# Six or eight rounded pieces of the second matrix beside the first layer of the first batch

## The chip, the cores and the metric

The kernel runs on one core of one Trainium2 chip. The metric is device time in microseconds of one execution; lower is better. All data are float32 except the two weight matrices, which arrive as float64.

## The reference

Eight batches of 448 rows pass through attention with 12 heads of 64, with normalised q and k, and then through two matrix products with a function between them.

```python
def _attn_ref(q, k, v, g_q, g_k):
    q_n, k_n = (rmsnorm(q, g_q), rmsnorm(k, g_k))
    scores = scale * np.matmul(q_n, k_n.transpose(0, 1, 3, 2))
    ...
    attn = attn / (np.sum(attn, axis=-1, keepdims=True) + 1e-09)
    return np.matmul(attn, v).astype(np.float32)

def _moe_ref(x, w_in, w_out):
    h = x @ w_in
    g = h - np.tanh(h)
    return (g @ w_out).astype(np.float32)
```

Here `x` is the attention output as 3584 x 768, `w_in` is 768 x 2048 and `w_out` is 2048 x 768.

## The kernel before

**Steps and batches.** One attention step handles two heads of one batch: 48 steps in all, six for each batch. While the attention of a batch is worked on, the two layers of the batch before it run beside it. The layers are a generator (`mlp`, L1273) that yields after each matmul; the attention code calls `run` (L1300) with a number of nanoseconds at fixed points of a step, and so many matmuls are written into the program there. `first_slot` (L1326) writes the steps of batch 0, `early_slot` (L1366) those of batch 1, beside which the first batch's layers run, and `slot` (L1394) the rest. The order within each engine's queue is the order of these calls; no scheduler changes it.

**The layers of batch 0.** The first layer (`hidden`, L865, through `products`, L813) multiplies by a scheme of seven products for each of four sets of weight blocks: 28 products of six matmuls of 128 x 224 each, in the order p = 1, 5, 6, 2, 3, 7, 4 within a set. Weight blocks 0, 1, 2 and 4 of a set are the weights themselves; blocks 5, 6, 3 and 7 are sums and differences of them, made on VectorE by `combine` (L354, the instructions of L356). The second layer of batch 0 (`project_first`, L1228) is plain: six groups of 16 matmuls of 128 x 448, counted by m from 0 to 95. The group is k = m // 16 and the row of the second matrix is f = m % 16. Groups k = 0 to 2 (below `HC`) use one half of the second matrix, groups 3 to 5 the other.

**Pieces of the weights.** The two float64 matrices are read as pairs of 32-bit words and rounded to float32 on the core, in 32 pieces of 768 KB: 16 of the first matrix (`CF`), then 16 of the second. Pieces 16 to 23 hold the half that the second layer's groups 0 to 2 need; row f needs piece 16 + f // 2. A piece passes through these steps, each on its own engine:

- `weight_load` (L278) issues its load on SyncE: four transfers at L289 for the first matrix, one at L293 for the second. Three buffers named `w_raw` take turns, so the load of piece n waits until piece n - 3 has been rounded.
- `round_weight_a` (L68): two ScalarE instructions, L71 and L72.
- `round_weight_b` (L75): three VectorE instructions, L78, L79 and L82.
- `round_weight_c` (L87): two GpSimd instructions at L92, one for each half of the piece; for the second matrix a half is one row f.

`weight(to)` (L320) rounds on until piece `to` - 1 has had its ScalarE part. For each piece n it issues `round_weight_a` of n, then `settle` (L335), which issues the VectorE and GpSimd parts of the piece before, then further loads, then up to two writes of finished blocks to DRAM (`keep_step`, L368, L371). `keep_w_out` (L392, L387) writes the rounded pieces of the second matrix back to DRAM as well.

**When pieces are due.** In the first layer the list `due` (L799) says for each of the 28 products how far the rounding must have come when the product is written (`product`, L822). If nothing is due, a pending VectorE and GpSimd part is settled and one block is written. In the second layer a formula in L1244 says it for each of the first 48 matmuls. Eight pieces are due before the first product (`EARLY`), 16 after 14 products, 24 after 28 products, and 32 after the first 48 matmuls of the second layer.

**What shares the queues.** A step of `early_slot` writes, in this order: the totals of the softmax (L696, with the reciprocal L701), scores of two chunks (L569) with their exponentials `p` (L575), the loads of v, a stretch of the layers, transposes of k and q (L467, L471) with their copies kT and qT on ScalarE (L469, L475) and two squarings (L132, L133), the loads of q and k, another stretch of the layers, scores of the last keys with the exponentials `p_last`, the values (L623, L673) with the division (L765), scores of one more chunk with the exponentials `p_full`, and then the norms (L142 to L144) and L454 between further stretches of the layers. Score banks are five in number and are used in turn, so the transposes use the bank of the totals again, and the second bank of the `p_full` scores is the first of `p_last`. The layers add their own work: tanh at L888, subtractions at L889 on VectorE or GpSimd, bank readers at L908 to L924, and in `project_first` a copy at L1264, a transpose at L950 and four output stores at L955.

Of the kernel before, what the change touches and what calls it, by code (L numbers as in the profile page):

```python
# [67 lines left out]
def round_weight_a(nc, raw, dst):  # L68

    lo, hi = raw[:, :, 0], raw[:, :, 1]  # L70
    nc.scalar.activation(dst, hi.bitcast(F32), AF.Abs, scale=2.0**-16)  # L71
    nc.scalar.mul(lo, lo.bitcast(U32), 2.0**-29)  # L72
# [74 lines left out]
def bounded_path(tc, ctx, q, k, v, moe_w_in, moe_w_out, out, g_col, ident, ones, half_ones, neg_half, early):  # L147
# [23 lines left out]
    CD, CF = DM // P, DFF // P  # L171
# [5 lines left out]
    EARLY, PIECES = 8, 2 * CF  # L177
    HS = S // 2
    HC, HF = CD // 2, CF // 2
    SETS = CF // 4  # L180
# [8 lines left out]
    def pool(name, **kw):  # L189
        return ctx.enter_context(tc.tile_pool(name=name, **kw))  # L190
# [23 lines left out]
    def mm_bank():  # L214
        return bank_of("mm")
# [48 lines left out]
    def w_out_row(f, i):  # L264
        return w_half[i][f // 2][:, f % 2]
# [35 lines left out]
    def weight_dst(n):  # L301
        return weight_piece(n)[2].rearrange("p f n -> p (f n)")
# [11 lines left out]
    def load_weights(to):  # L314

        while done[0] < min(to, PIECES) and place_free(done[0]):
            weight_load(done[0])
            done[0] += 1

    def weight(to):  # L320

        while done[1] < min(to, PIECES):
            n = done[1]
            keep_step(0, {CF - 4: 0, CF: 1, CF + HF: SETS - 1}.get(n, -1))
            round_weight_a(nc, raws[n], weight_dst(n))
            settle(n)
            done[1] = n + 1
            load_weights(n + (3 if n < EARLY - 3 else 4))
            if kept[1] < kept[0] and n >= 4 * kept[0] + 2:
                keep_weights()  # L330
            keep_step(2)
        if done[1] == PIECES:
            settle(PIECES)

    def settle(to):  # L335
        for n in range(done[2], to):
            round_weight_b(nc, raws[n], weight_dst(n))
            finish_weights(n + 1)
# [22 lines left out]
    def keep_weights():  # L361
        j = kept[1]
        to_keep.extend((j, p) for p in ORDER)
        kept[1] = j + 1
# [3 lines left out]
    def keep_step(count, all_of=-1):  # L368
        while to_keep and (count > 0 or to_keep[0][0] <= all_of):
            j, p = to_keep.pop(0)  # L370
            nc.sync.dma_start(out=w_in_dram[j, p].rearrange("p (f n) -> p f n", f=2), in_=built(j, p))  # L371
            count -= 1

    def combine_w_out(f):

        a11, a21 = (w_out_row(f, i) for i in range(2))
        a12, a22 = (w_out_row(f + HF, i) for i in range(2))
        t = [ring_slot() for _ in range(2)]
        s3, s1, s2, s4 = (t[i // 2][:, i % 2 * HALF : (i % 2 + 1) * HALF] for i in range(4))
        nc.vector.tensor_tensor(out=s1, in0=a21, in1=a22, op=ALU.add)  # L380
        nc.vector.tensor_tensor(out=s3, in0=a11, in1=a21, op=ALU.subtract)
        nc.vector.tensor_tensor(out=s2, in0=s1, in1=a11, op=ALU.subtract)
        nc.vector.tensor_tensor(out=s4, in0=a12, in1=s2, op=ALU.subtract)
        late["keep"].append(lambda: [keep_factors(3 + 2 * i, 2, f, t[i]) for i in range(2)])
# [7 lines left out]
    def keep_w_out(n):  # L392

        if not CF <= n < PIECES:
            return
        f, i, src = weight_piece(n)
        if f >= HF or i == 0:
            blk = i + 1 if f >= HF else 0
            for r in range(2):
                keep_factors(blk, 1, f % HF + r, src[:, r])  # L400
# [18 lines left out]
    def ring_load(to):  # L419

        for n in range(len(ring_tiles), min(to, len(ring_steps))):
            b, layer, j, p = ring_steps[n]
            t = ring_tiles[ring_steps[n]] = ring_slot()
            if layer == 0:
                assert kept[1] > j
                nc.sync.dma_start(out=t[:, : 2 * HALF], in_=w_in_dram[j, p])
            elif layer == 2 and p == 0:
                nc.sync.dma_start(out=t, in_=w_out_dram[:, BLOCKS[j], HC - 1].rearrange("p f d -> p (f d)"))
            elif layer == 2:
                n = min(2 * HB, 7 * HB - 2 * (p - 1) * HB)  # L430
                at = 2 * (p - 1) * HB
                nc.sync.dma_start(out=t[:, :n], in_=inner_dram[j][:, at : at + n])
            else:
                nc.sync.dma_start(out=t, in_=w_out_dram[:, BLOCKS[p], j].rearrange("p f d -> p (f d)"))
# [361 lines left out]
    late = {}  # L796


    due = [EARLY + (CF - EARLY) * (m + 1) // (7 * SETS // 2) for m in range(7 * SETS // 2)]  # L799
    due += [CF + HF * (m + 1) // (7 * SETS // 2) for m in range(7 * SETS // 2)]  # L800
    assert len(due) == 7 * SETS and due[-1] == CF + HF

    def part(name):
        if name == "th" and "blocks" in late:
            late["turn"] = (late.get("turn", 0) + 1) % 3
            if late["turn"] == 0:
                return late["blocks"].tile([P, 2, HS], F32, name="th_more")
        return tp.tile([P, 2, HS], F32, name=name)
# [134 lines left out]
    def store(b, n, y, o=None):  # L943

        if o is None:
            o = part("th").rearrange("p f s -> p (f s)")
        nc.vector.transpose(out=o, in_=y if b >= FIRST else y.rearrange("r (c p) -> r p c", c=NCH))  # L950

        def issue():
            for i in range(P // BL):
                d = n * P + i * BL
                nc.sync.dma_start(  # L955
                    out=out[b * S : (b + 1) * S, d : d + BL].rearrange("(j t) d -> t j d", t=BL),
                    in_=o[i * BL : (i + 1) * BL].rearrange("t (j d) -> t j d", d=BL),
                )

        late["out"].append([1 if b >= PAIRED else 2, issue])  # L960

    def step_out(by=1):
        for entry in late["out"]:
            entry[0] -= by
        while late["out"] and late["out"][0][0] <= 0:
            late["out"].pop(0)[1]()
# [261 lines left out]
    def project_first(b):  # L1228

        g = late["g"]  # L1230
        for fn in late["todo"]:
            fn()
        late["todo"] = []
        keep_step(0, SETS - 1)
        took = 4 * S / ENGINE_NS
        for m in range(CD * CF):
            k, f = m // CF, m % CF
            n = (k + HC) % CD
            if f == 0:
                bank = mm_bank()  # L1240
            if f == CF // 2:
                step_out(2)
            if k < HC:
                weight(CF + HF + HF * (m + 1) // (HC * CF))  # L1244
            elif m < HC * CF + 2:
                keep_w_out(PIECES - 2 + m - HC * CF)
            elif (m - HC * CF) % 4 == 0 and m - HC * CF <= 4 * HF:
                for fn in late["keep"]:
                    fn()
                late["keep"] = []  # L1250
                combine_w_out((m - HC * CF) // 4 - 1)
            elif m == CD * CF - 12:
                ring_load(2)
                for fn in late["keep"]:
                    fn()
            elif m == CD * CF - 10:
                ring_load(4)
            nc.tensor.matmul(  # L1258
                bank[:, :S], lhsT=w_out_row(f, n // HC)[:, n % HC * P : (n % HC + 1) * P], rhs=g[:, f, :],
                start=(f == 0), stop=(f == CF - 1),  # L1260
            )
            if f == CF - 1:
                y = part("s2").rearrange("p f s -> p (f s)")
                nc.scalar.copy(out=y, in_=bank[:, :S])  # L1264
                store(b, n, y)
            yield took
        wp_stack.close()
        late["blocks"] = pool("blocks", bufs=1)
        late["second"] = pool("second", bufs=1)
        late["tg"] = single_stack.enter_context(tc.tile_pool(name="tg", bufs=1))  # L1270
        late["inner"] = inner_steps()
# [415 lines left out]
def kernel(  # L1687
# [77 lines left out]
    with tc.If(bounded) as cmp:  # L1765
        with ExitStack() as arm, tc.manual_schedule():
            bounded_path(tc, arm, q, k, v, moe_w_in, moe_w_out, out, g_col, ident, ones, half_ones, neg_half, early)
# [34 lines left out]
```

## Time and profile before

| what | us |
|---|---|
| median of three runs | 1359.16 |
| lowest and highest run | 1357.87, 1359.49 |
| the profiled execution, its own time | 1356.19 |
| its span, first to last instruction | 1354.4 |
| TensorE matmul busy in the span | 1317.9 |
| VectorE, GpSimd, ScalarE busy | 949.1, 775.1, 556.9 |

The profile is of one execution, and instruction times in it count from the start of its span. Its own time is 1.8 us longer than the span, and it is 2.97 us shorter than the median of the three runs. In that execution the first layer of batch 0 begins at 76.8 us, its last product ends at 173.1 us, and the second layer runs from 176.4 us; its 49th matmul begins at 225.6 us.

In the stretches that the change touches, the engines were busy as follows:

| stretch, us | TensorE | VectorE | ScalarE | GpSimd | DMA share |
|---|---|---|---|---|---|
| 76 to 132 (first half of the first layer) | 49.1 of 56.0 | 53.4 | 32.2 | 33.6 | 0.81 |
| 132 to 176.4 (second half) | 44.4 of 44.4 | 41.7 | 25.1 | 34.8 | 0.89 |
| 176.4 to 221.3 (first half of the second layer) | 44.9 of 44.9 | 36.1 | 29.1 | 30.1 | 0.89 |

A row of the timeline gives start, duration, engine, line, operation, output and input; a bracket at its end tells how long the engine had been idle before it, and which instruction or transfer ended that.

### The profile page before, as it was taken

To read this page: it belongs to the slowest core of one execution; us is meant where nothing else is said; L and a number is where in the kernel's file an instruction comes from. 1 tells how busy PE (TensorE), PEld (TensorE's weight loads), DVE (VectorE), ACT (ScalarE), POOL (GpSimd) and SP (SyncE) were. 2 spreads that over 40 slices of the span, in tenths; PEclk is the share of its full clock that TensorE was granted. 3 is DMA by queue.
4 is the path that set the end of the run, shared out by engine and by line. 5 is a ranking of instruction groups with operands and counts; after the bars stand their busy time and mean duration, and the time that the engine had idled before them with its cause. 6 is when DMAs were issued, how large, how long until landed. Compare 5 with 4: busy or idle time off the path is not lost.

```text
span 1354.4 us, 29206 instructions
## 1 busy us (share of the span) xinstructions
PE 1317.9 (97%) x11336; PEld 1029.0 (76%) x11336; DVE 949.1 (70%) x1393; ACT 556.9 (41%) x1326; POOL 775.1 (57%) x591
## 2 busy tenths in 40 slices
PE   7989999999999999999999999999999999999996
PEld 3467854478998878697778787778787888699985
DVE  4999978757855768587887576768786668434453
ACT  7856654344433454445322446354512264311100
POOL 4766766347846256626698235844699253712761
PEclk9999999999999999999999999999999999999999
DMA  7879889889999667476655867476645775365544
GB/s 172 197 198 266 254 256 254 249 247 280 335 302 274 169 157 182 107 192 151 162 145 138 197 169 179 110 180 163 168 139 139 160 194 158 107 163 178 171 143 84
DMA packets 371688, 253.54 MB, mean 187 GB/s; under 512 B 282196, under 2 KB 310228, under 8 KB 371540
## 3 DMA queue, kind: packets, MB, share of 16 engines
q1 hardware_dynamic: 371536, 251.57, 68.9%
q8 instruction: 92, 1.51, 0.5%
q14 instruction: 56, 0.46, 0.1%
q10 hardware_dynamic: 4, 0.00, 0.0%
HBM read 205.23 MB, written 46.27 MB: 186 GB/s over the span
## 4 chain that ended last, share of the span: by engine, by line
PE 84%; DVE 9%; DMA 2%; SPq 2%; issue 1%; ACT 1%; POOL 1%; DVEq 0%; ACTq 0%
PE mm L841 36%; PE mm L1094 23%; PE sc L569 9%; PE sc L635 6%; PE mm L1258 5%; DVE xT L762 1%; PE sc L673 1%; PE sc L623 1%; SPq L955 1%; PE mm L673 1%; DVE rows L613 1%; DMA w_f<-w_in 1%; DVE rows L606 1%; DVE rows L600 1%; DMA w_f<-w_inner 0%
## 5 line engine op out<-in xcount | busy, mean ns | idle before, releaser
L841 PE MATMUL mm<-xT,w_f 128*128 128x224 f32 x1296 | 264.0, 353 | 0.7 <-DVE s L912 0.7
L841 PEld LDWEIGHTS mm<-xT,w_f 128*128 128x128 f32 x1296 | 244.5, 190 | 6.4 <-issue 4.8
L569 PE MATMUL sc<-qT,kT 64*32 64x448 f32 (+1 forms) x3072 | 214.2, 499 | 2.9 <-ACT p_last L575 1.7
L841 PE MATMUL mm<-tt,w_f 128*128 128x224 f32 x1044 | 213.7, 356 | 0.8 <-DMA w_f<-w_in 0.2
L841 PEld LDWEIGHTS mm<-tt,w_f 128*128 128x128 f32 x1044 | 194.9, 190 | 19.1 <-issue 15.4
L523 POOL TENSOR_TENSOR rr_mine<-rr_mine,neg_half 128x28 f32<-128x28 f32 x33 | 160.6, 4868 | 2.7
L758 DVE TENSOR_TENSOR xT<-xT,sc 128x448 f32<-128x448 f32 x32 | 19.9, 622 | 176.8 <-PE sc L569 119.3
L889 POOL TENSOR_TENSOR gT<-s,th 128x448 f32<-128x448 f32 x44 | 56.1, 1277 | 145.3 <-ACT th L888 142.0
L1094 PE MATMUL mm<-u,w_f 128*128 128x224 f32 x672 | 136.5, 354 | 1.2 <-DVE sum_all L733 0.9
L1094 PE MATMUL mm<-gT,w_f 128*128 128x224 f32 (+1 forms) x480 | 133.0, 429 | 3.1 <-DVE acc L1101 3.0
L1094 PEld LDWEIGHTS mm<-u,w_f 128*128 128x128 f32 x672 | 126.1, 190 | 8.2 <-POOL u L1051 3.9
L569 PEld LDWEIGHTS sc<-qT,kT 64*32 64x32 f32 x3072 | 71.0, 106 | 70.4 <-issue 50.5
L1094 PEld LDWEIGHTS mm<-gT,w_f 128*128 128x128 f32 x480 | 90.2, 190 | 40.7 <-issue 34.2
L635 PE MATMUL sc<-p,v_nat 64*32 64x448 f32 x1120 | 110.5, 536 | 0.0
L1094 PE MATMUL mm<-g,w_f 128*128 128x224 f32 (+1 forms) x360 | 99.5, 428 | 1.1 <-DVE acc L1101 1.1
L725 ACT COPY sum_g<-sum 32x14 f32<-32x14 f32 x280 | 56.3, 201 | 106.1 <-DVE sum L717 100.3
L889 POOL TENSOR_TENSOR g<-s,th 128x448 f32<-128x448 f32 x24 | 30.6, 1278 | 108.2 <-ACT th L888 93.3
L575 ACT ACTIVATE p<-sc 128x448 f32<-128x448 f32 x132 | 71.7, 543 | 50.3 <-PE sc L569 42.4
L1094 PEld LDWEIGHTS mm<-g,w_f 128*128 128x128 f32 x360 | 67.9, 190 | 28.2 <-issue 26.2
L1258 PE MATMUL mm<-gT,w_out 128*128 128x448 f32 x192 | 74.4, 543 | 0.0
L1051 POOL TENSOR_TENSOR u<-gT 128x448 f32<-128x448 f32 x48 | 58.8, 1247 | 11.1 <-PE mm L1094 11.1
L144 POOL TENSOR_TENSOR rr<-rr,neg_half 112x8 f32<-112x8 f32 (+1 forms) x30 | 49.4, 1675 | 26.7 <-DVE rr L143 26.2
(196 smaller groups left out, 2427.9 us busy)
## 6 DMA issues: line engine op xcount, KB each, us to landing
w_f<-w_in SPq DMA_DIRECT2D x196, 384.0 KB, 3.5
w_f<-w_inner SPq DMA_DIRECT2D x63, 512.0 KB, 3.7
w_f<-w_out SPq DMA_DIRECT2D x42, 512.0 KB, 3.9
w_raw<-in_moe_w_out_dram SPq DMA_DIRECT2D x16, 768.0 KB, 5.6
w_in<-w_out SPq DMA_DIRECT2D x21, 384.0 KB, 5.1
qk_nat<-in_q_dram SPq DMA_DIRECT2D x132, 56.0 KB, 2.8
qk_nat<-in_k_dram SPq DMA_DIRECT2D x132, 56.0 KB, 2.3
g<-w_out SPq DMA_DIRECT2D x14, 512.0 KB, 5.1
```

What stands on the lines that cost most here:

```text
L144: nc.gpsimd.tensor_tensor(out=r, in0=r, in1=neg_half[:rows], op=ALU.pow)
L523: nc.gpsimd.tensor_tensor(out=mine, in0=mine, in1=neg_half[:, :1].to_broadcast([P, 2 * NJ]), op=ALU.pow)
L569: nc.tensor.matmul(tiles[h][i * BL : (i + 1) * BL, :n], lhsT=kT[r, c * P + at : c * P + at + BL], rhs=qT[r, first : first + n], start=True ...
L575: nc.scalar.activation(p[:, h, c if c < 2 else 0, :], tiles[h][:, :n], AF.Exp, scale=1.0 if rr is None else rr[:, 0, 2 * c + h : 2 * c + h ...
L635: nc.tensor.matmul(av[g][i * BL : (i + 1) * BL, :S], lhsT=v_nat[keys, h, c, m * BL : (m + 1) * BL], rhs=p[keys, h], start=first, stop=True ...
L673: nc.tensor.matmul(av[n][r : r + BL, :HS], lhsT=v_nat[:, h, c, m * BL : (m + 1) * BL], rhs=p[c][:, h, n * HS : (n + 1) * HS], start=False, ...
L725: nc.scalar.copy(out=acc[h * BL : (h + 1) * BL, g], in_=part[g * BL : (g + 1) * BL, h * NJ : (h + 1) * NJ])
L841: nc.tensor.matmul(bank[:, f * HS : (f + 1) * HS], lhsT=w[:, c * width + f, :], rhs=moving[p](c), start=(first and f == 0 and c == 0), sto ...
L889: eng.tensor_tensor(out=g[:, rows, cols], in0=h, in1=th, op=ALU.subtract)
L1051: nc.gpsimd.tensor_tensor(out=u[:, half], in0=a[:, half], in1=z[:, half], op=ALU.subtract)
L1094: nc.tensor.matmul(bank[:, :n], lhsT=w(i), rhs=mv, start=(first and i == 0), stop=(i == len(moving) - 1), skip_group_check=not first,)
L1258: nc.tensor.matmul(bank[:, :S], lhsT=w_out_row(f, n // HC)[:, n % HC * P : (n % HC + 1) * P], rhs=g[:, f, :], start=(f == 0), stop=(f == C ...
```

## The change

Two lists of due times change. In the first layer the 14 pieces from the ninth on are spread evenly over the 28 products, so that 22 pieces are due at its end where 24 were. In the second layer a new list, `behind`, takes the place of the formula: ten pieces are due in its first 48 matmuls where eight were. For the first 16 matmuls the list also holds the rounding ahead of the rows: at matmul m it is at least 19 + m // 2.

```diff
-    due = [EARLY + (CF - EARLY) * (m + 1) // (7 * SETS // 2) for m in range(7 * SETS // 2)]
-    due += [CF + HF * (m + 1) // (7 * SETS // 2) for m in range(7 * SETS // 2)]
-    assert len(due) == 7 * SETS and due[-1] == CF + HF
+    SOME = HF - 2
+    due = [EARLY + (CF - EARLY + SOME) * (m + 1) // (7 * SETS) for m in range(7 * SETS)]
+    assert due[-1] == CF + SOME and due[7 * (SETS - 1) - 1] > CF
+    behind = [max(CF + m // 2 + 3, CF + SOME + (2 * HF - SOME) * (m + 1) // (HC * CF)) for m in range(CF)]
+    behind += [CF + SOME + (2 * HF - SOME) * (m + 1) // (HC * CF) for m in range(CF, HC * CF)]
...
             if k < HC:
-                weight(CF + HF + HF * (m + 1) // (HC * CF))
+                weight(behind[m])
             elif m < HC * CF + 2:
```

Here EARLY is 8, CF 16, HF 8, HC 3 and SETS 4. Pieces 0 to 10 are due where they were. Piece 11 is due at product 7 where it was due at 6, piece 16 at product 17 where it was at 15, piece 21 at product 27 where it was at 24, with products counted from 0. Pieces 22 and 23 were due at products 26 and 27 and are now due at matmuls 4 and 9 of the second layer; piece 24 was due at matmul 5 and is now due at 12, piece 25 at 11 and now at 14, and piece 31 stays at 47. The matmuls and their order are the same in both kernels.

## The prediction, on record before the result

> **What bounds the kernel now.** I read the page's busy shares first, then the chain of work that ended last in order of time, then the instructions around the change engine by engine. "Round a", "b" and "c" of a piece are lines 71 and 72 (ScalarE), 78 to 82 (VectorE) and 92 (GpSimd); a(25) is round a of piece 25.
>
> ```profile
> PE 1317.9 (97%) x11336; PEld 1029.0 (76%) x11336; DVE 949.1 (70%) x1393; ACT 556.9 (41%) x1326; POOL 775.1 (57%) x591
> ```
>
> TensorE is the bound nearly everywhere, so only its few stalls can be won or lost. In the stretch of the change the chain runs through VectorE up to 120.8 us and through TensorE after it (start, us, what):
>
> ```profile
> 109.53 1.78 DVE w_f L82
> 111.31 0.88 DVE w_f L356
> 112.21 1.66 DVE w_f L356
> ...
> 116.39 0.48 DVE w_out L78
> 116.89 0.57 DVE w_out L79
> 117.48 0.96 DVE w_out L82
> 118.44 0.87 DVE w_f L356
> 119.31 1.48 DVE rs L701
> 120.83 0.66 PE sc L467 x4
> ...
> 130.51 1.72 PE sc L569 x16
> ```
>
> The reciprocal L701 frees the bank that the transposes L467 need; TensorE stood still 2.32 us for it (its own row says so), because rounding b of piece 12 and three combinations L356 were ahead. The scores at 130.51 took 1.72 us where the same 16 took 0.92 at 98.00: their bank waited for an exponential behind a(15). From 132 us to the end of the first batch no row of TensorE shows idle before it until 275 us. What keeps that so is thin:
>
> ```profile
> 188.21 0.92 ACT L71 ACTIVATE w_out<-w_raw 128x768 f32<-128x768 f32 x1
> 189.02 1.05 ACT L72 ACTIVATE w_raw<-w_raw 128x768 int32<-128x768 uint32 x1
> 189.90 0.53 ACT L1264 COPY s<-mm 128x448 f32<-128x448 f32 x1
> 190.34 0.77 ACT L575 ACTIVATE p_last<-sc,rr 128x224 f32<-128x224 f32 x2
> ...
> 199.86 0.92 ACT L71 ACTIVATE w_out<-w_raw 128x768 f32<-128x768 f32 x1 [3.15 <-DMA w_raw<-in_moe_w_out_dram]
> ```
>
> Here a(25) runs without waiting and the exponentials p_last follow; a(27) at 199.86 waits for its load. The transfers, as SyncE issues them:
>
> ```profile
> 188.56 0.37 SPq L293 DMA_DIRECT2D w_raw<-in_moe_w_out_dram  x1
> 189.05 0.93 SPq L103 DMA_DIRECT2D qk_nat<-in_q_dram  x2
> ...
> 192.68 1.12 SPq L387 DMA_DIRECT2D w_out<-w_out  x2
> 193.97 1.15 SPq L293 DMA_DIRECT2D w_raw<-in_moe_w_out_dram  x1
> ```
>
> Load 26 at 188.56, six loads of q and k, two writes, load 27 at 193.97, used at 199.86: 11.3 us from one load's issue to the use of the next.
>
> **What the Trainium skill says.** "PSUM — Partial Sum Buffer", Engine vs sequencer instructions: the queues of ScalarE, VectorE and GpSimd are strict FIFO. The trace agrees: at 222.06 a(31) starts after 3.39 us of waiting for its load, and p_last, whose scores were done at 221.85, follows only at 224.17. "SBUF — State Buffer", Who interferes with whom: VectorE in a two-port mode or with two SBUF inputs and GpSimd lock each other out of a shared port pair. The trace agrees: L79 takes 0.56 us alone and 1.26 beside a GpSimd row, a half of round c 1.0 and up to 1.87. "DMA: Bandwidth & Descriptors", Anatomy of one DMA: 2.0 us plus bytes over 436 GB/s (fitted to another issuing path), an estimate of 3.8 us for a piece of 768 KB; the trace says 4.6 least, 5.6 median, 9.4 most from issue to landing, and decides.
>
> **The change part by part.** TensorE's own order is the same in both builds; all moves are on the other queues. Nothing is added or removed in all: each moved piece takes with it its load on SyncE, two ScalarE rows (1.8 us), three VectorE rows (2.1, up to 3.8 beside GpSimd), two GpSimd rows (2.0 to 3.3) and, for the second matrix, two writes. Up to the sixth product nothing moves; each later piece of the first 22 moves back by 1 to 3 products, and 22 and 23 leave the first layer.
>
> 1. *Gain at the transposes of 120.83.* Rounding b of piece 12 (116.39 to 118.44, 2.05) goes behind L701, and one of the three combinations (0.87 at least). L701 ends at 120.8 - 2.9 = 117.9 at the latest; TensorE is ready at 118.5. The wait of 2.32 us goes; late next are TensorE's own products. Cover: 0.6 us.
>
> 2. *Gain at the scores of 130.51.* a(15) goes behind p_last and p_full. p_last is then ready at about 128.0, where the scores come at 128.1 (130.51 - 2.3). Gain 1.72 - 0.92 = 0.8. Together -3.1 us.
>
> 3. *Hidden part, 132 to 176 us.* Seven pieces instead of eight; DVE 41.7, ACT 25.1 and POOL 34.8 of 44.4 us were busy, and TensorE did not wait. Moved with them past VectorE's and GpSimd's other rows are the combinations of set 3; the first is still some 10 us ahead of its product. On SyncE loads of v, q and k now stand before loads 15, 16 and 21; they have a whole step of some 30 us to land. The next reciprocal (149.58, needed at 151.7) gets more room. I cost this part at nothing; if that cover is gone, a late piece or reciprocal costs what the stall of 120.83 cost, up to 2.3.
>
> 4. *Loss at the first third of the second layer.* Four pieces, 22 to 25, are now issued in its first 16 products instead of two. Let T be the start of the transposes after the eighth product (182.53 before). a(23) now stands behind kT, qT and two squarings that need these transposes. In the next third such a group let a piece start at T + 2.64 (216.93 - 214.29). Then 0.9 (L71), b 0.56 + 0.56 + 0.96 = 2.1, and c in two halves of 1.0 to 1.6: done at T + 6.7 and T + 7.7 to 8.3. The products of rows 14 and 15 want them at T + 5.4 and T + 6.2: a wait of 1.5 to 2.1 us.
>
> 5. *Loss at the scores after it.* Load 24 must wait until round c of piece 21 frees the buffer. With U the end of the hidden products (T = U + 9.4): on GpSimd the power pair takes U to U + 3.3; three subtractions L889 follow, the last of which needs a tanh behind L454 (2.0), four exponentials (2.1) and itself (0.5), U + 6.3; it ends at U + 7.6 to 8.0; c(21) takes 2.0 to 2.6 (the 2.62 of 160.63). So load 24 is issued at T + 0.2 to T + 1.2; before it went out 9.6 us ahead of T. In the new SyncE order the six q and k loads and two writes stand between loads 24 and 25, as between 26 and 27 above: +11.3, a(25) starts at T + 11.5 to 12.5. Behind it on ScalarE wait L1264 and p_last: 1.67 + 0.45 + 0.40 = 2.5, first p_last ready at T + 14 to T + 15. The second scores bank is p_last's, wanted at T + 10.4 (192.93 - 182.53). Points 4 and 5 together cost 3.6 to 4.6 us with these landings, 2.5 with the shortest and 8 and more with the longest. I take 4.6, since rounding b of 21 and 22 runs just beside those GpSimd rows.
>
> 6. *Loss in the next third.* Load 29 (206.08 before, ahead of the output stores) falls behind four stores that need the bank finished at V (206.07 before): copy 0.5, transpose 0.9, stores 2.2, two writes 1.1, with waits V + 5.0. Load 31 goes out about when 29 has landed (each transfer waits for the eighth before it in this build): V + 11.7. It lands 5.7 later (216.30 to 222.06), then 2.5 as above: p_last at V + 19.9, wanted at V + 18.6 (224.63 - 206.07). Cost 1.3; zero to 4 with the landings. After that the pieces are done by 230 us, before their products, and the delay rides to the end.
>
> **Sum.** -3.1 + 4.6 + 1.3 = +2.8 us on the profiled execution: 1356.19 (span 1354.4, 1.8 around it) becomes 1359.0. The median of the runs lies 2.97 above that execution: 1359.16 + 2.8 = 1362.0.
>
> **Rivals.**
> *The loads come in time (ends not slower).* Loads 24 and 25 decide: if a(25) starts by T + 9.5, p_last is ready when the scores, already 1.6 late through point 4, come. That needs 8.3 to 9.3 us for the pair in place of 11.3; the shortest landing twice is 9.2, so c(21) must also end early. DMA engines were busy 0.83 in 176 to 201, so they have some room; the measured pair speaks against it. -3.1 + 1.6 + 0.2: 1357.9.
> *The gain alone.* Rounding a of 23 finds ScalarE so early that nothing waits: 1356.1. Against it: the order kT before a(23) is in the build.
> *The loads pile up.* 201 to 222 had DMA busy 0.97; landings of 7 to 9 us for loads 24, 25, 28 and 31 add 2 to 3 each twice on the way: +5.5 to +8, about 1366.
> *It doesn't do what it says:* the built order shows the pieces moved; no chance is given.
>
> **Chances.** The forecast 0.50 (1360 to 1364.5, of which 0.30 above the bound), pile-up 0.20, in time 0.18 (0.14 within), gain alone 0.12 (0.10 faster). The bound of 0.2% is 2.7 us, about what a measurement of this kernel can tell from no change. Slower 0.50, within 0.36, faster 0.14. The range from 1356.4 to 1367.0 leaves out some 0.08 below and 0.06 above.
>
> **What would show it.** Right: no idle of TensorE before the transposes near 118.5; an idle at the products of rows 14 and 15 with releaser GpSimd L92; one at the scores ten us after the transposes with releaser ScalarE p_last, and there a(25) with a long DMA wait; load 24 issued just after c(21). Wrong: a(25) without DMA wait; a new wait in 132 to 176; a stall that stays at 120.

## The result, and the profile after

The changed kernel takes 1361.9 us (median of 13 runs, 1360.12 to 1364.81). In the same series the kernel before took 1357.38 us (13 runs; the three shown above, with a median of 1359.16, are the first of them). The ratio is 1.0032, 95% interval 1.0025 to 1.0040: 4.3 us slower, 3.4 to 5.4. Here and below, microseconds beside a ratio are the ratio's; differences of medians can be up to 1.2 us off from them. The profiled execution has a span of 1358.7 us, against 1354.4.

The change did take away the stall that it met first. TensorE's rows after the change, with start, duration, engine, line, operation and, in brackets, the idle time before the row and who ended it:

```profile
118.15 0.60 PE L467 MATMUL sc<-ident,qk_nat 128*128 128x128 f32 x4
119.02 0.60 PE L471 MATMUL sc<-ident,n 112*128 112x112 f32 x4 [0.27 <-ACT p L575]
...
184.36 1.02 PE L1260 MATMUL mm<-gT,w_out 128*128 128x448 f32 x2 [0.30 <-POOL w_out L92]
186.91 1.99 PE L1260 MATMUL mm<-gT,w_out 128*128 128x448 f32 x4 [1.53 <-POOL w_out L92]
188.84 0.61 PE L569 MATMUL sc<-qT,kT 64*32 64x224 f32 x16
...
192.16 0.94 PE L569 MATMUL sc<-qT,kT 64*32 64x448 f32 x2
194.93 0.98 PE L569 MATMUL sc<-qT,kT 64*32 64x448 f32 x14 [1.83 <-ACT p_last L575]
195.84 1.02 PE L1260 MATMUL mm<-gT,w_out 128*128 128x448 f32 x2
```

The transposes L467 start at 118.15 with no bracket; before, they started at 120.83 behind 2.32 us of idle time. The loss follows 65 us later: two products wait for GpSimd's L92 (each product of the second layer is two matmuls in these rows; the one at 184.36 is that of row 13, for piece 22, and 186.91 begins rows 14 and 15, for piece 23), and 14 of the 16 scores for p_last. The sum of such waits from 135 to 285 us (engine, what waited, releaser, us in all, times, longest):

```profile
PE sc L569 <- ACT p_last L575: 2.5, 2, 1.8
PE mm L1260 <- POOL w_out L92: 1.8, 2, 1.5
PE sc L569 <- ACT p L575: 0.4, 1, 0.4
```

The kernel before has only the last of the three there, with 0.5. Where p_last was kept shows on ScalarE and SyncE. First ScalarE, then SyncE's queue:

```profile
186.20 0.90 ACT L71 ACTIVATE w_out<-w_raw 128x768 f32<-128x768 f32 x1 [2.53 <-DMA w_raw<-in_moe_w_out_dram]
...
192.45 0.90 ACT L71 ACTIVATE w_out<-w_raw 128x768 f32<-128x768 f32 x1 [4.55 <-DMA w_raw<-in_moe_w_out_dram]
193.26 0.86 ACT L72 ACTIVATE w_raw<-w_raw 128x768 int32<-128x768 uint32 x1
194.03 0.50 ACT L1266 COPY s<-mm 128x448 f32<-128x448 f32 x1
194.44 0.78 ACT L575 ACTIVATE p_last<-sc,rr 128x224 f32<-128x224 f32 x2
```

```profile
181.05 0.37 SPq L293 DMA_DIRECT2D w_raw<-in_moe_w_out_dram  x1
181.54 0.93 SPq L103 DMA_DIRECT2D qk_nat<-in_q_dram  x2
...
185.12 1.45 SPq L387 DMA_DIRECT2D w_out<-w_out  x2
186.72 0.40 SPq L293 DMA_DIRECT2D w_raw<-in_moe_w_out_dram  x1
```

Before, a(25) ran at 188.21 with no wait and p_last at 190.34. Now load 24 goes out at 181.05, load 25 at 186.72, a(25) starts at 192.45 after 4.55 us of waiting, and p_last stands behind it. The chain of waits of the changed kernel runs through just these (start, us, what):

```profile
186.72 5.70 DMA w_raw<-in_moe_w_out_dram
...
193.26 0.86 ACT w_raw L72
194.12 0.41 ACT s L1266
194.53 0.35 ACT p_last L575
...
194.93 0.98 PE sc L569 x14
```

A bracket shows less than a wait costs, because ends of matmuls are modelled. So I count delays from starts of rows. T is the start of the transposes after the eighth product of the second layer; before, the first scores start at T + 7.00 and the 17th product 4.24 us after them, and the 49th product 31.83 us after the 17th. What exceeds that is delay. "Second batch" is the start of the first eight of its products (277.80 before).

| us | before | after | change |
|---|---|---|---|
| products after the scores near 130 us | 132.16 | 129.10 | -3.06 |
| T | 182.53 | 179.30 | -3.23 |
| first scores (rows 14 and 15 waited) | 189.53 | 188.84 | +2.54 |
| 17th product (p_last waited) | 193.77 | 195.84 | +2.76 |
| 49th product (next third waited) | 225.60 | 229.10 | +1.43 |
| second batch | 277.80 | 281.30 | +3.50 in all |
| last long run of products | 1260.72 | 1264.89 | +4.17 in all |

The balance is -3.23 + 2.54 + 2.76 + 1.43 = +3.50. Another 0.7 us in all is lost later, where the change has no instruction: the changed kernel stands 3.1 us behind near 770 us and 4.2 near 1090 us.

### The profile page after: what moved, and what is told of

Its sections match the earlier page's. It is cut to its first block, busy times and chain, and to the rows that moved or that the text cites. A ratio compares the mean times of both kernels' runs of the same rounds, so it can differ in the third digit from the quotient of the medians.

```text
span 1358.7 us, 29209 instructions
## 1 busy us (share of the span) xinstructions
PE 1321.9 (97%) x11336; PEld 1030.2 (76%) x11336; DVE 951.3 (70%) x1393; ACT 557.9 (41%) x1326; POOL 771.2 (57%) x591
## 4 chain that ended last, share of the span: by engine, by line
PE 79%; DVE 9%; DMA 3%; SPq 2%; ACT 2%; issue 2%; POOL 1%; DVEq 0%; ACTq 0%; POOLq 0%
PE mm L843 35%; PE mm L1096 23%; PE sc L569 8%; PE sc L635 5%; PE mm L1260 4%; DVE xT L762 2%; DMA w_raw<-in_moe_w_in_dram 1%; DVE rows L613 1%; PE sc L623 1%; DMA w_raw<-in_moe_w_out_dram 1%; DVE rows L606 1%; DVE rows L600 1%; DVE sum_T L710 1%; PE sc L673 1%; ACT p L575 1%
## 5 line engine op out<-in xcount | busy, mean ns | idle before, releaser
L891 POOL TENSOR_TENSOR gT<-s,th 128x448 f32<-128x448 f32 x44 | 55.6, 1269 | 140.5 <-ACT th L890 140.0
L891 POOL TENSOR_TENSOR g<-s,th 128x448 f32<-128x448 f32 x24 | 30.3, 1264 | 108.8 <-ACT th L890 93.8
L1260 PEld LDWEIGHTS mm<-gT,w_out 128*128 128x128 f32 x192 | 35.4, 190 | 39.7 <-issue 34.1
```

The source lines that it names most:

```text
L891: eng.tensor_tensor(out=g[:, rows, cols], in0=h, in1=th, op=ALU.subtract)
L1260: nc.tensor.matmul(bank[:, :S], lhsT=w_out_row(f, n // HC)[:, n % HC * P : (n % HC + 1) * P], rhs=g[:, f, :], start=(f == 0), stop=(f == C ...
```

## The experiments

Ratios are to the kernel before on the same chip (1359.16 us for the first four, 1357.37 for the next four).

### Each half of the change alone

Here the first layer ends with 24 pieces as before and the second layer is untouched. The first 14 products have the due times of the change (15 pieces), and nine pieces are left for the other 14:

```diff
+    due = [EARLY + (m + 1) // 2 for m in range(7 * SETS // 2)]
+    due += [CF - 1 + (HF + 1) * (m + 1) // (7 * SETS // 2) for m in range(7 * SETS // 2)]
...
+                weight(CF + HF + HF * (m + 1) // (HC * CF))
```

> The first layer's list as changed for its first 14 products (15 pieces due), then nine pieces in the other 14, so that 24 are due at its end; the second layer is left as before. Theory (gain and loss are two separate things): the 3.2 us gained by 130 us stay, the transposes of the second layer start at about 179.3 against 182.5 before, and no exponential p_last is waited for. Rows 14 and 15 of the second layer may wait up to 2.5, since round c of piece 23 ended only 0.2 us before its product in the kernel before and hangs on its load. In all 0.5 to 3.2 us faster than before. Rival (the rounding costs TensorE time wherever it lies): the gain is given back in the second half of the first layer, transposes not before 181.5, and the time within 1 us of before.

Measured: 1357.0 us, ratio 0.9985 (0.9977 to 0.9992), 2.0 us faster than before. There is no delay at rows 14 and 15, at p_last or in the next third; the second batch starts at 276.08 (-1.72). The gain at 120 and 130 us can thus be had without the loss. It is not kept whole: the transposes of 118.15 come at 118.73 (TensorE was as far behind at 111 us already), and the scores of 158.72, which take 0.98 in the changed kernel, take 2.02 here, because a piece waited for its load ahead of p_last. ScalarE in this kernel:

```profile
157.57 0.97 ACT L71 ACTIVATE w_out<-w_raw 128x768 f32<-128x768 f32 x1 [0.85 <-DMA w_raw<-in_moe_w_out_dram]
158.44 0.95 ACT L72 ACTIVATE w_raw<-w_raw 128x768 int32<-128x768 uint32 x1
159.28 0.75 ACT L575 ACTIVATE p_last<-sc,rr 128x224 f32<-128x224 f32 x2
```

So nine pieces in the second half of the first layer do cost something, 1.0 us here; the rival had that part right. Eight cost little: the same scores took 1.16 us in the kernel before and 0.98 in the run with seven pieces of eight below, which also has eight pieces in that half.

The other half alone has the old first 14 due times and the new list in the second layer:

```diff
+    due = [EARLY + (CF - EARLY) * (m + 1) // (7 * SETS // 2) for m in range(7 * SETS // 2)]
+    due += [CF + SOME * (m + 1) // (7 * SETS // 2) for m in range(7 * SETS // 2)]
```

> The first 14 products as in the kernel before (16 pieces due), six pieces in the other 14, and the second layer as changed (ten pieces). Theory: no gain at 118 to 131 us, the whole loss in the second layer: waits of TensorE of about 1.8 at rows 14 and 15, 3.5 at the scores after them and 1.4 a third later, 6.7 us in all, so 5 to 7 us slower than before. Rival (the waits come from TensorE being 3.2 us ahead of the transfers, and are the gain given back): waits of 3.5 or less in all, and at most 3.5 us slower than before.

Measured: 1366.56 us, ratio 1.0057 (1.0042 to 1.0071), +7.7 us. The stall at 120.83 is back (2.61), and the delays are those of the changed kernel to 0.05 us: 2.54, 2.78, and 1.47 in the next third once 1.59 us are taken off that TensorE lost there at half clock (32 products took 13.88 us in place of 12.29). The gain and the loss are two things in two places. The timed halves, -2.0 and +7.7, come to 5.7 where the whole change has 4.3; their intervals, 1 and 2 us to either side, cover the difference.

### Is it p_last?

In the two steps concerned, TensorE's scores for p_last and its exponentials are written ahead of the eight products, so p_last stands ahead of the piece in ScalarE's queue:

```diff
+        if s in (9, 10):
+            scores(s + 1, KF)
         run(gap)
-        if has(s + 1):
+        if has(s + 1) and s not in (9, 10):
             scores(s + 1, KF)
```

> The changed kernel, but in the two steps beside the first half of the second layer the scores of the last keys and their exponentials p_last are written ahead of the second stretch of the layers, so that on ScalarE they stand before rounding a of pieces 23 to 25 and 30 to 31 and not behind it. Theory (the loss is p_last standing behind a piece whose load is late): the waits for p_last of 3.5 and 1.4 go, the wait at rows 14 and 15 grows by the 0.8 us that p_last takes on ScalarE, to about 2.6; the 49th matmul of the second layer starts near 225 against 229.1 in the changed kernel and 225.6 before; about 4 us faster than the changed kernel, within 1.5 of before. Rival (ten pieces are more than the engines and transfers carry in that time): the waits move to other instructions, and the time stays within 1.5 us of the changed kernel.

Measured: 1360.12 us, ratio 1.0006 (0.9997 to 1.0015), level with the kernel before. TensorE in this kernel:

```profile
187.26 2.00 PE L1260 MATMUL mm<-gT,w_out 128*128 128x448 f32 x4 [1.66 <-POOL w_out L92]
...
192.13 0.98 PE L569 MATMUL sc<-qT,kT 64*32 64x448 f32 x16
193.04 1.40 PE L1260 MATMUL mm<-gT,w_out 128*128 128x448 f32 x3
```

The wait for L92 is there (1.66); the 16 scores are one row again, with no bracket. The 49th product starts at 225.09, 4.0 us ahead of the changed kernel: about the 2.76 + 1.43 of p_last. The second batch starts at 277.87, 3.4 us ahead. Of the 0.6 us lost in between, 0.5 lie at the row sums L696 of 237.31, which took 1.10 us in place of 0.58: VectorE's L613, whose result they read, ended only at 237.78.

### Is it piece 23?

Piece 23 is due at the eighth product, ahead of the transposes, and load 25 stays where it was:

```diff
+    behind[7:9] = [CF + HF] * 2
...
-            load_weights(n + (3 if n < EARLY - 3 else 4))
+            load_weights(n + (3 if n < EARLY - 3 else 2 if n == CF + HF - 1 else 4))
...
                 weight(behind[m])
+                if m == 9:
+                    load_weights(CF + HF + 2)
```

> The changed kernel with one move: piece 23 is due at matmul 7 of the second layer in place of 9, so that its rounding a stands ahead of kT, qT and the squarings on ScalarE; loads 24 and 25 stay on the same sides of the q and k loads. Theory: the wait at rows 14 and 15 shrinks from 1.8 to about 0.8, but the exponential p_last still comes after load 25, so that the wait at the scores grows by the same and the matmul after them starts at 195.8 as in the changed kernel: no change in time, within 0.5 us in the profile. Rival (the two waits add): about 1 us faster than the changed kernel.

Measured: 1367.02 us, ratio 1.0049 (1.0034 to 1.0063), +6.7 us: a miss for both sides. The wait at rows 14 and 15 did shrink (0.93 in the bracket, delay 2.11), but the two writes of a piece went ahead of the q and k loads in SyncE's queue, and load 25 went out 1.0 us later than in the changed kernel. SyncE here:

```profile
181.43 1.00 SPq L387 DMA_DIRECT2D w_out<-w_out  x2
...
183.85 2.43 SPq L117 DMA_DIRECT2D qk_nat<-in_k_dram  x2
...
187.74 0.48 SPq L293 DMA_DIRECT2D w_raw<-in_moe_w_out_dram  x1
```

The scores then waited 3.07 us in the bracket, and TensorE ran at half clock from 194.5 to 201.3 us, which cost 1.94 us in the 32 products behind alone. What the rows gained, p_last took, and more: where p_last comes last, the products ahead of it have slack.

### Is it the queue ahead of load 25?

The six loads of q and k of this one step are issued after the second stretch of products:

```diff
-        if has(s + 4) and not by_blocks(s + 4):
+        if has(s + 4) and not by_blocks(s + 4) and s != 9:
             load(s + 4, "qk")
         run(gap)
+        if s == 9:
+            load(s + 4, "qk")
```

> The changed kernel, with the six loads of q and k of one step issued after the loads of pieces 25 to 27 and not between those of 24 and 25; nothing else moves. Theory (load 25 is late because it stands in SyncE's queue behind those six and two writes, though its buffer was free at 184.31): load 25 goes out near 184.4 in place of 186.72, a(25) starts 1.5 to 2.3 earlier, p_last too, and the wait of 3.5 us at the scores shrinks to 1.2 to 2.0. The time is 1.5 to 2.3 us below the changed kernel, about +2.3 us on the kernel before. Rival (the transfers share the DMA engines, 0.8 to 0.9 busy there, so an earlier issue only means a longer landing): a(25) within 0.7 us of where it was, +3.6 to +4.6 on the kernel before. The wait at rows 14 and 15 stays at 1.8 in both.

Measured: 1360.95 us, ratio 1.0026 (1.0016 to 1.0037), +3.5 us; the second batch starts at 280.10, 1.2 us ahead of the changed kernel. SyncE and then TensorE in this kernel:

```profile
181.30 0.37 SPq L293 DMA_DIRECT2D w_raw<-in_moe_w_out_dram  x1
181.72 1.00 SPq L387 DMA_DIRECT2D w_out<-w_out  x2
184.57 0.37 SPq L293 DMA_DIRECT2D w_raw<-in_moe_w_out_dram  x1
```

```profile
187.16 2.86 PE L1260 MATMUL mm<-gT,w_out 128*128 128x448 f32 x4 [1.54 <-POOL w_out L92]
189.95 1.00 PE L569 MATMUL sc<-qT,kT 64*32 64x224 f32 x16
...
193.80 0.98 PE L569 MATMUL sc<-qT,kT 64*32 64x448 f32 x16
```

Load 25 goes out 3.27 us after load 24 in place of 5.67, a(25) starts at 189.58 in place of 192.45, and the first wait at p_last is gone: more than I expected, and against the rival that the landing would grow. The traces also show how the queue holds load 25 back. As the prediction says of this build, a transfer waits for the eighth before it. In none of the twelve traces does one of SyncE's go out before the eighth ahead of it has landed, wherever that landing is recorded. In the changed kernel the second of the two writes is the eighth behind load 24: it goes out at 186.19, just when that load has landed (a(24) starts at 186.20), and load 25 follows it. With two writes alone between the loads nothing waits for that landing. But the four products at 187.16 took 2.86 us where they take 2.00: TensorE's clock was halved just behind the wait of 1.54. By the starts of rows that stretch cost 0.86 + 0.53 = 1.4 us, so in this execution it ate half of the 2.76. The mechanism is shown in the trace; the timed gain over the changed kernel, some 0.8 us, lies within the two intervals.

### Can the piece step behind p_last?

A lead of two pieces in place of three in the new list:

```diff
-    behind = [max(CF + m // 2 + 3, CF + SOME + (2 * HF - SOME) * (m + 1) // (HC * CF)) for m in range(CF)]
+    behind = [max(CF + m // 2 + 2, CF + SOME + (2 * HF - SOME) * (m + 1) // (HC * CF)) for m in range(CF)]
```

> The changed kernel with a lead of two in place of three in the second layer's list, which moves only the rounding of piece 25: it stands behind the exponentials p_last and p_full, not ahead of L1266 and p_last; SyncE's order is the same. Theory (p_last is late only because it stands behind a(25), which waits for its load): the wait at the scores of the first third goes altogether, 3.5 us; the rows 14 and 15 still wait 1.8; the next third still waits 1.0 to 2.0 or a little more, since load 28 follows round c of piece 25. At 280 us the kernel stands level with the kernel before to +1; time 0 to +2 us on the kernel before, 2.5 to 4 us below the changed one. Rival (the late transfers are the cost, wherever the piece stands in the queue): the wait comes back at p_last of the next third, 3 us or more in place of 1.4, and the time is within 1.5 us of the changed kernel.

Measured: 1363.08 us, ratio 1.0035 (1.0021 to 1.0049), +4.8 us: my theory missed and the rival held. The first wait at p_last did go (17th product at 193.17, 2.7 us ahead of the changed kernel). But rounding is staged: when a(25) moves, b(24) moves with it, and GpSimd's c(24) falls behind the attention rows L793. GpSimd, then TensorE, in this kernel:

```profile
195.64 1.38 POOL L793 TENSOR_TENSOR tt<-xT,tt 128x224 f32<-128x224 f32 x1
196.98 3.67 POOL L92 TENSOR_TENSOR w_out<-w_out,w_raw 128x384 int32<-128x384 int32 x2
```

```profile
223.96 0.94 PE L569 MATMUL sc<-qT,kT 64*32 64x448 f32 x2
227.66 1.74 PE L569 MATMUL sc<-qT,kT 64*32 64x448 f32 x14 [2.77 <-ACT p_last L575]
```

Here c(24) starts at 196.98 where the changed kernel has it at 190.07. Load 27 needs the buffer of piece 24 and goes out at 200.68 in place of 192.09, and every load to 31 is late in turn. The next third waits 2.77 in the bracket in place of 0.63, and its delay is 4.33 us in place of 1.43, of which 0.76 is half clock in the 14 scores; 0.76 more of half clock falls in the products behind them. So 2.1 of the 2.76 us had only been passed on through the three buffers, and half clock took the rest.

### Seven pieces of eight

```diff
-    SOME = HF - 2
+    SOME = HF - 1
```

> SOME = HF - 1: 23 pieces due in the first layer, nine in the second. Theory: up to 150 us the order is that of the changed kernel, so the gain at the transposes and scores near 120 and 130 us stays (2.9 to 3.1 us). Everything from piece 22 on stands one place earlier: load 25 goes out after round c of 22 near 181 and ahead of the q and k loads, a(25) near 186.5, p_last with no wait; rows 14 and 15 wait 0 to 0.5; the next third has three pieces in place of four and waits 0 to 1.0. Up to 1 us may be lost in the second half of the first layer, where 7.5 pieces stand and not seven. Sum -1.5 to -3 us on the kernel before, ratio 0.998 to 0.999. Rival (any piece moved to the second layer costs there, in proportion): half the loss of the changed kernel's 6.7, -3.1 + 3.3 = about 0, within 0.8 us of the kernel before.

Measured: 1355.01 us, ratio 0.9984 (0.9975 to 0.9993), 2.2 us faster than before. TensorE:

```profile
185.63 1.02 PE L1260 MATMUL mm<-gT,w_out 128*128 128x448 f32 x2 [0.20 <-POOL w_out L92]
...
222.96 0.98 PE L569 MATMUL sc<-qT,kT 64*32 64x448 f32 x14 [0.16 <-ACT p_last L575]
```

T is 179.16, the whole gain of 3.37; the delays are 0.42, 0.25 and 0.97. Load 24 goes out at 175.92, before T, and load 25 at 182.17, ahead of the q and k loads. One piece more in the first layer takes away three quarters of the loss (1.6 us are left of 6.7) and none of the gain, so the loss is not in proportion to the pieces moved. The rival's "about 0" lies outside the interval.

The same with TensorE's scores ahead, as above:

> The kernel with 23 pieces in the first layer, and in the two steps concerned TensorE's scores for p_last and the step's exponentials written ahead of the eight products before them, so that p_last stands ahead of the piece in ScalarE's queue. Theory: if with 23 pieces there is no wait at p_last left, this adds nothing: within 0.7 us of the run with 23 pieces alone. If a wait of 0.5 to 1.5 us is left there (in the next third above all), it goes, and this run is that much faster, near -3 on the kernel before. Rival: taking TensorE's scores ahead delays the products and what follows from them, 0.5 to 1 us slower than 23 pieces alone.

Measured: 1354.85 us, ratio 0.9977 (0.9966 to 0.9989). No wait at p_last is left. In the trace it stands 1.0 us ahead of seven pieces alone at the second batch; in the timed runs the two can't be told apart. It is the fastest median measured, and only by 0.16 us.

### The changed kernel in two more executions

The changed kernel, unedited, for the 0.7 us left over and the half clock.

> The changed kernel once more, unedited, for a second profiled execution. Two things are open: what the 0.7 us are that its first profile lost after 490 us, where no instruction of the change stands, and whether the TensorE waits of 1.5 to 2.8 us near 185, 194 and 227 us are now and then followed by a stretch of some 3.4 us at half the granted clock, as they were in the runs with only the second layer's part, with piece 23 ahead, with the loads of q and k later and with piece 25 behind. Theory (the clock gate falls by chance of where its window lies): the instructions' waits come back within 0.2 us (1.8 at rows 14 and 15, 3.5 at the scores, 1.4 in the next third), while the stretches at half clock lie elsewhere or differ in number; a stretch behind one of the waits costs 1 to 1.7 us. Rival (the stretches belong to the kernel): same places, same number as in the first profile, two before 80 us and none behind the waits.

> The changed kernel a third time, with the same expectations as the second look: the same waits within 0.2 us; under the theory stretches at half clock that differ in place or number from the first two profiles, under the rival the same ones.

Measured: 1365.28 and 1361.98 us. The delays of the first third are 2.53 and 2.65 in one, 2.84 and 1.94 in the other, against 2.54 and 2.76; "within 0.2" was too tight for p_last. In the second execution the transposes near 118 us wait 0.55 us for L701 again, and TensorE ran at half clock from 197.1 to 200.5 us, behind the wait at p_last, and its next third lost 4.28 us in place of 1.43 (1.70 of it in the 32 products at half clock); in the third no such stretch followed, and it lost 1.87. The stretches are therefore not the kernel's own, as the theory had it. From the second batch to the last long run of products the three executions lost 0.7, 1.1 and 2.2 us on the kernel before. That part varies while the instructions stay the same, and the kernel before has one trace alone, while its 13 runs spread from 1355.95 to 1362.29; I have no cause for it.

## Why the prediction was right, and where its sizes were off

The sign, the places and the releasers held: +2.8 us was worked out, and +4.3 measured (3.4 to 5.4). That 1362.0 lies so near to 1361.9 is partly luck, for the median of three that it was added to lay 1.8 us above the median of all 13. On the profiled execution the sum was 1.5 short: 0.7 in points 4 and 5, 0.1 in point 6 and 0.8 after the second batch began, less 0.1 of greater gain.

- *Points 1 and 2, the gains.* -3.1 predicted, -3.06 measured. L701 now runs at 116.14 for 1.55 us, and at L467 TensorE's own products came last, as foreseen; the four transposes L471 after it then waited 0.27 us for an exponential of ScalarE. The cover of 0.6 us did not always suffice: L467 waited 0.55 in one of the three executions and in the run with seven pieces, and the last section shows what those two had in common.
- *Point 3, the hidden part at nothing.* It held: T moved by 0.17 more, to the good. The edge lies between eight pieces, which cost 0.2 us or less, and nine, which cost 1.0 in the run with the first layer alone.
- *Point 4, rows 14 and 15.* 1.5 to 2.1 predicted, 2.54 measured. Round a of 23 started at T + 2.63, as worked out (T + 2.64). The term that was short is round b, taken as 0.56 + 0.56 + 0.96. VectorE of the changed kernel:

```profile
182.88 0.56 DVE L78 TENSOR_SCALAR w_out<-w_out 128x768 f32<-128x768 f32 x1 [1.04 <-ACT w_out L71]
183.48 1.25 DVE L79 TENSOR_SCALAR w_out<-w_out 128x768 int32<-128x768 int32 x1
184.76 0.96 DVE L82 SCALAR_TENSOR_TENSOR w_out<-w_raw,w_out 128x768 int32<-128x768 int32 x1
```

  L79 took 1.25 beside c(22), which ran on GpSimd until 184.31; L78 took no longer than alone beside the same rows. The prediction had that price (1.26 beside a GpSimd row) and did not charge it here. This did not make the sum short, though: the 17th product came when p_last was ready, and by that account a shorter delay at the rows would only have made TensorE wait longer there.
- *Point 5, the scores.* The two points together were taken at 4.6 and cost 5.30. The 4.6 stands for a(25) at T + 12.5, the latest time worked out; it began at T + 13.15, and these 0.65 us are nearly all that the two points were short. The pair of loads took 11.4 us (181.05 to 192.45), 11.3 predicted. The term mis-sized is the issue of load 24: it went out at T + 1.75, outside T + 0.2 to T + 1.2, as the third subtraction L891 took 1.84 and c(21) 2.62 beside VectorE's round b. The run with the q and k loads later shows that the queue ahead of load 25 was the reason for the pair's length; the run with the scores ahead shows that p_last was what TensorE lacked. That p_last can't overtake a(25) is the strict order of ScalarE's queue that the Trainium skill states ("PSUM — Partial Sum Buffer", Engine vs sequencer instructions): p_last ran 1.99 us after a(25) began (2.13 before), although a(25) came 4.24 us later.
- *Point 6, the next third.* 1.3 predicted, 1.43 measured. Load 31 went out at 219.89, V + 11.75 where V + 11.7 was predicted (V is 208.14 here), and landed in 5.69 (5.7 predicted). But the path to it was another, so that this agreement is luck. The four stores ahead of load 29 belong to the bank finished near 189 us and did not wait for V: they went out at 205.80, and load 29 at 210.74, V + 2.6 in place of V + 5.0. It had landed 4.5 us before load 31 went out. What load 31 waited for was its buffer: a(28), behind the copy L1266 of the bank finished at V, the norm L454 and four exponentials on ScalarE, and then c(28) on GpSimd, which ended at 219.87:

```profile
212.59 0.93 ACT L71 ACTIVATE w_out<-w_raw 128x768 f32<-128x768 f32 x1
217.37 2.50 POOL L92 TENSOR_TENSOR w_out<-w_out,w_raw 128x384 int32<-128x384 int32 x2 [1.55 <-ACT w_raw L72]
219.89 0.37 SPq L293 DMA_DIRECT2D w_raw<-in_moe_w_out_dram  x1
```

  The other two executions gave 1.87, and 4.28 with a stretch at half clock.
- *"The delay rides to the end."* It did, with 0.7 us on top that is not explained.

Of the rivals, "the loads come in time" failed at load 25 and "the gain alone" at rows 14 and 15. The landings of loads 25 and 31 took 5.7 us, so nothing piled up on this path; what came nearest to that rival was the run with piece 25 behind, whose lateness was passed on through the buffers.

## What to carry to other kernels

Before moving background work from one stretch to another, look there for the first thing the bound engine needs that stands behind it in a queue. Here that was p_last behind one rounding, and its price was set by when a load could be issued: the release of a buffer plus what else stood in the DMA queue, and whether that had to wait for an earlier landing. Such a price has a threshold: seven pieces of eight gained 2.2 us where six lost 4.3. Moving only the late step behind its victim is not enough when the same buffers turn round: most of the lateness came back one third later.

## What was unexpected of the hardware

A wait of TensorE can cost more than its length. In five profiled executions the granted clock fell to half at or just behind the new waits. The clock column (third from the end) of the run with the q and k loads later, by stretches of 1 us:

```profile
186.00:187.00 1.00, 0.00 (x0) 0.00 (x0) 0.00 (x0) 0.61 (x1) 0.91 (x1) 1.00 1.19 369
...
188.00:189.00 1.00, 1.00 (x2) 0.52 (x2) 0.97 (x2) 0.09 (x1) 0.08 (x1) 0.50 1.00 386
...
192.00:193.00 1.00, 1.00 (x28) 0.70 (x24) 0.81 (x1) 0.41 (x2) 0.86 (x2) 1.00 1.05 356
```

The traces show what this goes with. In each of the twelve, all changes of the clock lie whole multiples of 3.413 us apart (in this run 95.53 and 187.69 us, 27 times). So windows of that length run through an execution, and the clock changes at their borders alone. All the kernels here, the one before too, have the same wait of some 2.5 us for VectorE near 91 us. In nine of the twelve traces at least 2.22 us of it lay in one window, and the next window was at half clock. In the other three (second layer alone, seven pieces, changed kernel in its second execution) a border divided it, at most 1.97 us lay in one window, and the clock stayed. The kernel before and the run with seven pieces show both cases:

| execution | window, us | TensorE idle in it, us | clock in it | clock in the next window |
|---|---|---|---|---|
| before | 88.40 to 91.81 | 2.54 | 1.00 | 0.50 |
| seven pieces | 86.98 to 90.39 | 1.97 | 1.00 | 1.00 |

The waits of the second layer divide in the same way:

| execution | wait shown just before, us | idle in one window, us | at half clock, us |
|---|---|---|---|
| piece 25 behind p_last | 2.77 | 2.59 | 3.4 |
| piece 23 ahead | 3.07 | 1.86 | 6.8 |
| q and k loads later | 1.54 | 1.83 (with the short wait before) | 3.4 |
| second layer alone | 1.78 | 1.78 | 3.4 |
| changed kernel, second execution | 1.72 | 1.72 | 3.4 |
| scores ahead | 1.66 | 1.66 | none |
| changed kernel, third execution | 1.54 | 1.64 (with the short wait before) | none |
| changed kernel, first execution | 1.83 | 1.55 | none |

The border value, between 1.66 and 1.72 us here and between 1.97 and 2.22 near 91 us, is thus not one number, and near 64 us 1.50 us were followed by a stretch in one trace; why it differs is not shown, and the idle times rest on modelled ends.

The Trainium skill ("TensorE: Matmul & The Clock Gate", Part 1: The HAM clock gate) says that the clock halves after an idle window of about 3.4 us and comes back after a busy one, and that the windows are 3413 ns long and run freely. The traces agree on the length and on the free run. They do not agree that a whole window must be idle: 1.72 to 2.59 us of one were enough. A stretch of 3.4 us cost 1.4 to 1.7; the prediction did not charge for any.

This also touches point 1. Its cover of 0.6 us was read from an execution that had the stretch near 92 us. The two executions with the new order that lacked it, the second of the changed kernel and the one with seven pieces, are the two in which the transposes near 118 us waited 0.55 us for L701.
